# A group's state update moved directly ahead of its local products, in one unit, and the copy of its transposed k moved up to the transposes

## The chip, the cores and the metric

The program runs on one core of a Trainium2 chip. The metric is device time in microseconds (us), median of the runs shown. Five engines work side by side, each taking its own queue of instructions in order: TensorE (PE, matmuls; PEld is its weight loads), VectorE (DVE), ScalarE (ACT), GpSimd (POOL) and SyncE (SP, which here issues most DMA transfers). An instruction that waits holds everything behind it in its queue.

## The reference

Inputs q, k, v and f_logit have the shape (4, 8, 768, 48): batch, heads, tokens, head width. A gated recurrence runs over the tokens, and two MLPs with 384 inputs, 2048 hidden values and 384 outputs follow on all 3072 tokens.

```python
f = 1.0 / (1.0 + np.exp(-f_logit))
for t in range(S):
    state = f[:, :, t, :, None] * state + np.einsum('bhd,bhe->bhde', k[:, :, t], v[:, :, t])
    y[:, :, t] = np.einsum('bhd,bhde->bhe', q[:, :, t], state)
...
h = x @ w_in;  g = softplus(h);  x = g @ w_out           # first MLP
h = x @ w_in2; g = h * tanh(softplus(h)); x = g @ w_out2  # second MLP
```

## The kernel before

**The recurrence in groups.** The 768 tokens are cut into 6 chunks of 128. A group `g` is one chunk of one batch entry with all 8 heads, taken as 4 pairs; there are 24 groups, `g = 4 * chunk + batch`. For each group the kernel does, in this order:

- `a_scan`, `a_inv`, `a_q`, `a_k`, `a_decay` (lines 253 to 304, DVE and ACT): the running products of the gates, and q, k and the old state scaled by them (L256, L279 and L280, L286, L292, L300);
- `a_scores` (L322, PE): k times q within the chunk, into two PSUM banks; `a_mask` (L335, DVE): the causal mask, one bank at a time;
- `a_turn` (L346, PE): four transposes of the scaled k into a PSUM bank; `a_turned` (L352, ACT): the copy of that bank to the tile `kn`, which has one buffer;
- `a_out` (L390 and L399, PE): the local products (masked scores times v, L390) and the old state times q (L399); `a_outed` (L426 and L433, ACT): the copies of the result out of PSUM;
- `a_state` (L361, PE): `kn` times v, eight small matmuls; `a_stated` (L370, DVE): the new state, old plus product. The groups of the last chunk have no state to hand on, so 20 of the 24 groups have these two;
- `a_load` (SP): q, k and v of the group after next.

All PSUM banks that the steps of a group use are taken in turn from two (`ps_a`, tags a0 and a1, one buffer each): two for the scores, then one for each of the other PE steps in the order in which they are written.

**The MLPs in units.** A unit `(layer, k, f)` is one tile of 512 tokens (`k`, six of them) and one slice of 128 of the hidden values (`f`, sixteen), so there are 96 units per layer. `m_h` makes the hidden values (L483: nine matmuls of 512 columns, each product of two floats split into high and low parts, xh, xl and a two-part weight; the first eight slices of the first tile go whole, L469). Softplus or mish runs on ACT and DVE (L512 to L533), the result is split again (L498 `ghi`, L503 `glo`), and `m_o` multiplies it back (L613: six matmuls with `ghi`, three with `glo`; L603 whole). `m_o` follows three units behind `m_h`. The weights are split on the core too: `split_w` (L139 to L151) reads two loads of a slice (`raw`, L128 and the same bytes shifted, L129) and writes the high part at L147 and the low part at L151. For the first layer's slices 8 to 15 this stands in the units just ahead of their use; slices 14 and 15 take over the staging tiles of slices 12 and 13, once these are split.

**What sets the order.** The recurrence is woven into the first 80 units: `plan_attn` hangs the steps of a group on hooks of three units in a row, `at(unit, place, step)`, and a unit runs its places in the order act0, pe1, dve1, (softplus), act, (softplus), dve2, (split, `m_o`), pe2. That is the order in which the program is written. For these units the queue of each engine is then laid out by the framework's scheduler, which takes ready instructions by that order with times of its own, so a moved step can change the order of other work as well. From unit 80 on the order of PE, DVE and ACT is as written. The first four groups stand in a list of their own (`HEAD`) ahead of all units.

Of the kernel before, what the change touches and what calls it, by code (L numbers as in the profile page):

```python
# [17 lines left out]
B, H, S, D = 4, 8, 768, 48  # L18
C = 128
NC = S // C  # L20
# [38 lines left out]
def recurrence__then__softplus_mish_mlps_kernel(  # L59
# [43 lines left out]
    act, dve, pe = nc.scalar, nc.vector, nc.tensor  # L103
# [549 lines left out]
    def at(i, place, fn, *args):  # L653
        hooks.setdefault((i, place), []).append(lambda: fn(*args))
# [16 lines left out]
    def plan_attn(g, i):  # L671

        at(i, "pe1", a_scores, g)
        at(i, "dve2", a_mask, g, 0)
        at(i, "dve2", a_mask, g, 1)
        at(i + 1, "pe1", a_turn, g)
        at(i + 1, "act", a_turned, g)
        at(i + 1, "pe2", a_out, g)
        at(i + 2, "act0", a_outed, g)
        if g < (NC - 1) * B:  # L680
            at(i + 2, "pe1", a_state, g)
            at(i + 2, "dve2", a_stated, g)
        if g + 2 < NC * B:
            at(i + 2, "dve2", a_load, g + 2)

    for k in range(1, n1):
        c, b0, nb = tiles[1][k]
        base = (k - 1) * NF
        for j in range(nb):
            g, i = c * B + b0 + j, base + 3 * j  # L690
            plan_attn(g, i)
            if g + 1 < NC * B:
                plan_prep(g + 1, i if j < nb - 1 else i + 3)
            else:
                at(i + 3, "dve1", judge)
        i = base + 3 * nb
        at(i, "act", a_fill, k)
        for kk in range(KD):
            at(i + 1 + kk, "dve1", split_x, (1, k), kk)
# [20 lines left out]
    for f in range(NF):  # L720
        if f >= READY:
            i = f - AHEAD
            at(max(i - EARLY, -1), "act0", load_w, 1, f)
            at(i, "dve1", whole_w if f < NAT else conv1, f)
        i = first + SPAN + (last - first - SPAN) * f // NF
# [15 lines left out]
    for step in LOADS.split():  # L741
        what, g = step[0], int(step[1:])
# [333 lines left out]
```

## Time and profile before

| | us |
|---|---|
| median of 3 runs | 948.49 |
| lowest and highest | 948.35 and 949.86 |
| the profiled execution | 948.94 |
| its span (first to last instruction) | 947.2 |

| engine | busy us | share of the span |
|---|---|---|
| PE | 922.5 | 97% |
| PEld | 727.1 | 77% |
| DVE | 784.7 | 83% |
| ACT | 738.2 | 78% |
| POOL | 29.5 | 3% |

A busy time is the union of an engine's instructions. Matmuls are pipelined: one is shown from its start to a modelled end, which lies past the start of the next. So time lost between matmuls without a wait doesn't show as idle time; it is read from the distance of one start to the next.

### The profile page before, as it was taken

To read this page: it belongs to the slowest core of one execution; us is meant where nothing else is said; L and a number is where in the kernel's file an instruction comes from. 1 tells how busy PE (TensorE), PEld (TensorE's weight loads), DVE (VectorE), ACT (ScalarE), POOL (GpSimd) and SP (SyncE) were. 2 spreads that over 40 slices of the span, in tenths; PEclk is the share of its full clock that TensorE was granted. 3 is DMA by queue.
4 is the path that set the end of the run, shared out by engine and by line. 5 is a ranking of instruction groups with operands and counts; after the bars stand their busy time and mean duration, and the time that the engine had idled before them with its cause. 6 is when DMAs were issued, how large, how long until landed. Compare 5 with 4: busy or idle time off the path is not lost.

```text
span 947.2 us, 13705 instructions
## 1 busy us (share of the span) xinstructions
PE 922.5 (97%) x4970; PEld 727.1 (77%) x4970; DVE 784.7 (83%) x1252; ACT 738.2 (78%) x1326; POOL 29.5 (3%) x84
## 2 busy tenths in 40 slices
PE   4999989999999999999999999999999999999996
PEld 4655767787777777877888888888888888888885
DVE  5999999998998998987676688788877877877875
ACT  3778897888688787867687588787878878877875
POOL 1000000000000000000012210000000000000000
PEclk9999999999999999999999999999999999999999
DMA  9699713454754756381038660200200101000001
GB/s 307 226 354 332 272 56 110 131 196 174 246 177 159 267 183 215 144 283 42 9 135 261 178 226 1 67 34 1 88 13 27 74 1 67 34 1 1 34 0 38
DMA packets 35117, 122.33 MB, mean 129 GB/s; under 512 B 4352, under 2 KB 7424, under 8 KB 35040
## 3 DMA queue, kind: packets, MB, share of 16 engines
q1 hardware_dynamic: 28704, 99.34, 30.5%
q0 software_dynamic: 6336, 22.02, 7.2%
q8 instruction: 41, 0.67, 0.3%
q14 instruction: 36, 0.29, 0.1%
HBM read 93.62 MB, written 26.74 MB: 127 GB/s over the span
## 4 chain that ended last, share of the span: by engine, by line
PE 88%; DVE 7%; issue 2%; ACT 2%; POOL 0%; POOLq 0%; ACTq 0%; DVEq 0%
PE po L613 40%; PE ps L483 39%; PE ps L322 2%; PE ps L390 2%; PE ps L399 2%; PE ps L361 1%; PE ps L346 1%; PE ps L469 1%; DVE d L526 1%; PE busy L767 1%; DVE gg L256 1%; DVE a L335 1%; DVE w L147 1%; DVE d L520 1%; DVE raw L176 0%
## 5 line engine op out<-in xcount | busy, mean ns | idle before, releaser
L483 PE MATMUL ps<-x,w 128*128 128x512 f32 x864 | 214.0, 392 | 0.0
L613 PE MATMUL po<-ghi,w 128*128 128x512 f32 x768 | 206.7, 400 | 0.0
L483 PEld LDWEIGHTS ps<-x,w 128*128 128x128 f32 x864 | 162.3, 188 | 37.0
L483 PE MATMUL ps<-xh,w 128*128 128x512 f32 x528 | 181.3, 398 | 2.5 <-DVE w L151 2.3
L613 PEld LDWEIGHTS po<-ghi,w 128*128 128x128 f32 x768 | 141.5, 189 | 31.7 <-ACT ghi L498 0.7
L613 PE MATMUL po<-g,w 128*128 128x512 f32 x504 | 126.0, 394 | 0.0
L483 PEld LDWEIGHTS ps<-xh,w 128*128 128x128 f32 x528 | 98.9, 188 | 28.5 <-issue 3.6
L547 ACT ACTIVATE l<-d 128x512 f32<-128x512 f32 x96 | 60.7, 633 | 73.4 <-DVE d L543 73.4
L613 PE MATMUL po<-glo,w 128*128 128x512 f32 x384 | 112.4, 392 | 0.0
L613 PEld LDWEIGHTS po<-g,w 128*128 128x128 f32 x504 | 94.9, 188 | 21.4
L483 PE MATMUL ps<-xl,w 128*128 128x512 f32 x264 | 103.6, 392 | 0.0
L512 ACT ACTIVATE e<-ps 128x512 f32<-128x512 f32 x96 | 57.2, 596 | 56.6 <-PE ps L483 46.4
L503 DVE TENSOR_TENSOR glo<-l,ghi 128x512 fp32r<-128x512 f32 x128 | 87.7, 685 | 14.2 <-ACT ghi L498 13.6
L543 DVE TENSOR_SCALAR d<-ps 128x512 f32<-128x512 f32 x96 | 66.3, 690 | 37.5 <-PE ps L483 37.4
L498 ACT CAST ghi<-l 128x512 fp32r<-128x512 f32 x128 | 78.2, 611 | 20.7 <-DVE l L533 20.2
L557 DVE SCALAR_TENSOR_TENSOR l<-d,l 128x512 f32<-128x512 f32 x96 | 66.5, 693 | 33.2 <-ACT l L550 33.1
L520 DVE SCALAR_TENSOR_TENSOR d<-d,e 128x512 f32<-128x512 f32 x96 | 65.7, 685 | 23.1 <-ACT d L514 23.0
L613 PEld LDWEIGHTS po<-glo,w 128*128 128x128 f32 x384 | 72.4, 189 | 16.0
L580 DVE TENSOR_TENSOR l<-ps,l 128x512 f32<-128x512 f32 x96 | 66.4, 692 | 9.6 <-ACT l L577 0.9
L526 DVE TENSOR_TENSOR d<-l,d 128x512 f32<-128x512 f32 x96 | 65.7, 685 | 2.6
L572 DVE SCALAR_TENSOR_TENSOR l<-d,l 128x512 f32<-128x512 f32 x96 | 65.4, 681 | 0.0
L514 ACT ACTIVATE d<-e 128x512 f32<-128x512 f32 x96 | 60.7, 632 | 1.7
(107 smaller groups left out, 1284.4 us busy)
## 6 DMA issues: line engine op xcount, KB each, us to landing
raw<-in_w_dram SPq DMA_DIRECT2D x32, 768.0 KB, 6.1
w2d<-wo SPq DMA_DIRECT2D x32, 384.0 KB, 2.7
w<-w2d POOLq DMA_DIRECT2D x32, 384.0 KB, 3.9
raw<-in_w_dram SPq DMA_DIRECT2D x16, 767.9 KB, 10.4
win<-in_w_dram SPq DMA_DIRECT2D x16, 767.9 KB, 7.2
qk<-in_qkT_dram SPq DMA_DIRECT2D x22, 448.0 KB, 4.8
x2d<-o SPq DMA_DIRECT2D x12, 768.0 KB, 5.2
x<-x2d POOLq DMA_DIRECT2D x12, 768.0 KB, 5.4
```

Source lines behind the costliest of these rows:

```text
L483: pe.matmul(ps, w, r, start=(i == 0), stop=(i == len(steps) - 1))
L498: act.copy(out=t["hi"], in_=t["g"])
L503: dve.tensor_tensor(out=t["lo"], in0=t["g"], in1=t["hi"].bitcast(F32), op=ALU.subtract)
L514: act.activation(out=d, in_=e, func=AF.Identity, bias=1.0)
L520: dve.scalar_tensor_tensor(out=d, in0=d, scalar=1.0, in1=t["e"], op0=ALU.subtract, op1=ALU.subtract)
L526: dve.tensor_tensor(out=d, in0=l, in1=d, op=ALU.subtract)
L543: dve.tensor_scalar(out=t["t"], in0=t["h"], scalar1=20.0, scalar2=None, op0=ALU.min)
L547: act.activation(out=t["l"], in_=t["t"], func=AF.Exp)
L557: dve.scalar_tensor_tensor(out=t["l"], in0=t["t"], scalar=-43.0, in1=t["l"], op0=ALU.max, op1=ALU.add)
L572: dve.scalar_tensor_tensor(out=t["l"], in0=t["t"], scalar=-1.0, in1=t["l"], op0=ALU.mult, op1=ALU.max)
L580: dve.tensor_tensor(out=t["l"], in0=t["h"], in1=t["l"], op=ALU.mult)
L613: pe.matmul(acc[c], w[layer, f][:, cols[c]], t[part], start=(f == 0 and part == "hi" and w is whi), stop=(f == NF - 1 and part == "lo"),)
```

## The change

Three hooks of `plan_attn` move. The copy `a_turned` goes from the place act to the place pe1 of the same unit, right behind the transposes. `a_state` goes from pe1 of unit i + 2 to pe2 of unit i + 1, ahead of `a_out`. `a_stated` goes from dve2 to dve1 of unit i + 2.

```diff
         at(i + 1, "pe1", a_turn, g)
-        at(i + 1, "act", a_turned, g)
+        at(i + 1, "pe1", a_turned, g)
+        if g < (NC - 1) * B:
+            at(i + 1, "pe2", a_state, g)
         at(i + 1, "pe2", a_out, g)
         at(i + 2, "act0", a_outed, g)
         if g < (NC - 1) * B:
-            at(i + 2, "pe1", a_state, g)
-            at(i + 2, "dve2", a_stated, g)
+            at(i + 2, "dve1", a_stated, g)
```

No instruction is added or removed. The two PSUM banks change hands in another order: the state now takes the second bank of the scores, and the local products take the bank of the transposes, where before it was the other way round.

On PE around the local products of a group (here group 7), before: the products (L390, L399), a whole `m_h` (L483), then the state's matmuls (L361).

```order
L390 MATMUL ps<-a,vt 64x128 x8
L399 MATMUL ps<-qk,sp 48x128 x8
L483 MATMUL ps<-xh,w 128x512
L483 MATMUL ps<-xl,w 128x512
L483 MATMUL ps<-xh,w 128x512 x2
L483 MATMUL ps<-xl,w 128x512
L483 MATMUL ps<-xh,w 128x512 x2
L483 MATMUL ps<-xl,w 128x512
L483 MATMUL ps<-xh,w 128x512
L361 MATMUL ps<-vt,kn 64x48
L361 MATMUL ps<-vt,kn 48x48
```

And on PE at the same group now (three more pairs of L361 stand where lines are left out):

```order
L613 MATMUL po<-ghi,w 128x512 x6
L613 MATMUL po<-glo,w 128x512 x3
L361 MATMUL ps<-vt,kn 64x48
L361 MATMUL ps<-vt,kn 48x48
...
L390 MATMUL ps<-a,vt 64x128 x8
L399 MATMUL ps<-qk,sp 48x128 x8
L483 MATMUL ps<-xh,w 128x512
```

The eight small matmuls have moved from behind `m_h` to directly ahead of L390. From group 8 on this is so at eleven groups; at group 8 itself one of the eight stands alone, three L613 ahead of the other seven.

The second place is on PE at the last slice of the first tile (unit (1, 0, 15)), whose weights are split just ahead of it. Before: the `m_o` of slice 12, the nine L483 of slice 15, the `m_o` of slice 13.

```order
L613 MATMUL po<-ghi,w 128x512 x6
L613 MATMUL po<-glo,w 128x512 x3
L483 MATMUL ps<-xh,w 128x512
L483 MATMUL ps<-xl,w 128x512
L483 MATMUL ps<-xh,w 128x512 x2
L483 MATMUL ps<-xl,w 128x512
L483 MATMUL ps<-xh,w 128x512 x2
L483 MATMUL ps<-xl,w 128x512
L483 MATMUL ps<-xh,w 128x512
L613 MATMUL po<-ghi,w 128x512 x6
L613 MATMUL po<-glo,w 128x512 x3
```

And on PE there now:

```order
L613 MATMUL po<-ghi,w 128x512
L613 MATMUL po<-glo,w 128x512 x3
L322 MATMUL ps<-qk 128x128
L483 MATMUL ps<-xh,w 128x512
L483 MATMUL ps<-xl,w 128x512
L613 MATMUL po<-ghi,w 128x512 x6
L483 MATMUL ps<-xh,w 128x512 x2
L483 MATMUL ps<-xl,w 128x512
L483 MATMUL ps<-xh,w 128x512 x2
L483 MATMUL ps<-xl,w 128x512
L483 MATMUL ps<-xh,w 128x512
L613 MATMUL po<-glo,w 128x512 x3
```

Six L613 of slice 13 now stand between the second and the third L483 of slice 15, and the scores of group 8 (L322) are spread over this stretch in pieces of one, two, four and one, where before all eight stood together.

The third place is DVE at the same slice, around the last L151 with output `w`, which writes the low weights of slice 15. Before:

```order
L457 TENSOR_TENSOR xl<-x,xh 128x512
L148 TENSOR_SCALAR raw<-w 128x768
L533 SCALAR_TENSOR_TENSOR l<-ps,d 128x512
L151 SCALAR_TENSOR_TENSOR w<-raw 128x768
L457 TENSOR_TENSOR xl<-x,xh 128x512
L503 TENSOR_TENSOR glo<-l,ghi 128x512
L520 SCALAR_TENSOR_TENSOR d<-d,e 128x512
L457 TENSOR_TENSOR xl<-x,xh 128x512
L526 TENSOR_TENSOR d<-l,d 128x512
L199 TENSOR_TENSOR w<-w_346,w 128x768
L533 SCALAR_TENSOR_TENSOR l<-ps,d 128x512
L256 SCALAR_TENSOR_TENSOR gg<-f,cap 112x516
```

And on DVE there now:

```order
L526 TENSOR_TENSOR d<-l,d 128x512
L256 SCALAR_TENSOR_TENSOR gg<-f,cap 112x516
L457 TENSOR_TENSOR xl<-x,xh 128x512
L147 TENSOR_TENSOR w<-raw 128x768
L533 SCALAR_TENSOR_TENSOR l<-ps,d 128x512
L148 TENSOR_SCALAR raw<-w 128x768
L457 TENSOR_TENSOR xl<-x,xh 128x512
L151 SCALAR_TENSOR_TENSOR w<-raw 128x768
L503 TENSOR_TENSOR glo<-l,ghi 128x512
L520 SCALAR_TENSOR_TENSOR d<-d,e 128x512
L457 TENSOR_TENSOR xl<-x,xh 128x512
```

A scan (L256) and a second L457 now stand ahead of that L151. Counted from the start of the queue, these two are all that DVE does more before it than it did; every other kind of instruction comes as often.

## Rows read from the trace of the kernel before

**Rows 1.** The page, busy time of each engine.

```profile
PE 922.5 (97%) x4970; PEld 727.1 (77%) x4970; DVE 784.7 (83%) x1252; ACT 738.2 (78%) x1326; POOL 29.5 (3%) x84
```

**Rows 2.** Stretches of 25 us: PE, PEld, DVE, ACT, POOL busy (instructions), PEclk, DMA, GB/s.

```profile
75.00:100.00 25.00, 25.00 (x139) 14.21 (x137) 25.00 (x43) 20.07 (x33) 0.11 (x1) 1.00 1.01 325
125.00:150.00 25.00, 23.01 (x130) 17.70 (x129) 23.65 (x40) 19.78 (x37) 0.11 (x1) 0.93 0.16 57
```

**Rows 3.** PE's waits: waiting line, releaser: us in total, times, longest us.

```profile
PE ps L483 <- DVE w L151: 2.3, 2, 1.8
```

**Rows 4.** Timeline of PE, around group 9's state, then between tiles: start, us, what.

```profile
163.97 0.50 PE L483 MATMUL ps<-xh,w 128*128 128x512 f32 x1
...
166.24 0.67 PE L361 MATMUL ps<-vt,kn 128*64 128x48 f32 x16
166.83 1.65 PE L613 MATMUL po<-ghi,w 128*128 128x512 f32 x6
...
169.01 0.39 PE L483 MATMUL ps<-xh,w 128*128 128x512 f32 x1
...
203.27 0.39 PE L483 MATMUL ps<-xh,w 128*128 128x512 f32 x1
...
205.33 1.54 PE L613 MATMUL po<-ghi,w 128*128 128x512 f32 x6
```

**Rows 5.** Timeline of PE in the head, local products behind each other.

```profile
28.84 0.86 PE L413 MATMUL ps<-a,vt 128*48 128x128 f32 x12
29.53 0.64 PE L390 MATMUL ps<-a,qkv 128*64 128x128 f32 x4
...
30.97 0.86 PE L413 MATMUL ps<-a,qkv 128*48 128x128 f32 x12
31.76 0.94 PE L409 MATMUL ps<-y,sel 128*128 128x128 f32 x6
```

**Rows 6.** Instructions on line L361 from 130 to 460 us.

```profile
L361 PE MATMUL ps<-vt,kn x192: 208/222/257, 146.2 to 371.0; 128*64 128x48 f32 x96, 128*48 128x48 f32 x96
```

**Rows 7.** DVE's waits from 45 to 130 us, all there are.

```profile
DVE glo L503 <- ACT ghi L498: 0.2, 1, 0.2
```

**Rows 8.** Timeline, DVE and PE, up to the last slice of the first tile.

```profile
59.44 1.22 DVE L256 TENSOR_TENSOR_SCAN gg<-f,cap 112x516 f32<-112x516 f32 x1
60.58 0.53 DVE L163 TENSOR_SCALAR raw<-raw 128x768 int32<-128x768 int32 x1
...
129.25 0.68 DVE L457 TENSOR_TENSOR xl<-x,xh 128x512 fp32r<-128x512 f32 x1
129.39 0.73 PE L483 MATMUL ps<-xh,w 128*128 128x512 f32 x2 [1.80 <-DVE w L151]
129.85 0.68 DVE L503 TENSOR_TENSOR glo<-l,ghi 128x512 fp32r<-128x512 f32 x1
...
131.30 2.77 PE L613 MATMUL po<-ghi,w 128*128 128x512 f32 x6
...
134.75 0.40 PE L483 MATMUL ps<-xh,w 128*128 128x512 f32 x1
```

**Rows 9.** Timeline, slice 15's load and its first reader; then that load's landing.

```profile
113.61 0.94 DVE L151 SCALAR_TENSOR_TENSOR w<-raw 128x768 fp32r<-128x768 int32 x1
115.00 0.42 SPq L129 DMA_DIRECT2D raw<-in_w_dram  x1
123.43 0.56 DVE L140 TENSOR_SCALAR raw<-raw 128x768 int32<-128x768 int32 x1
...
DMA to landing us min/median/max: 7.1/7.1/7.1
```

**Rows 10.** Timeline, group 15's transposes, local products and copy.

```profile
278.62 0.55 PE L346 MATMUL ps<-ident,qk 112*128 112x112 f32 x4
281.17 1.09 PE L390 MATMUL ps<-a,vt 128*64 128x128 f32 x16
281.34 0.53 ACT L352 COPY kn<-ps 128x448 f32<-128x448 f32 x1
```

## The prediction

> **What bounds the kernel now.** I read the page's busy times first. PE is busy 97% of the span, DVE 83%, ACT 78% [rows 1], so the time is PE's unless another engine holds it up. Next PE's waits: from 50 us on there is hardly one, and the largest is for DVE, 2.3 us for the low weights that L151 writes [rows 3]. The table of stretches says where: from 75 to 100 us PE and DVE are both full; from 125 to 150 PE loses 2 us of 25 and its granted clock is 0.93 [rows 2]. So there are two regimes. Up to about 130 us DVE runs without a gap (its only wait from 45 to 130 us is 0.2 us, [rows 7]), and PE's work behind the last weight split can't start before DVE is through. From there PE never waits, and only what PE itself does counts.
>
> The Trainium skill says the same of the measure ("Perfetto Trace Analysis", Identifying the Most-Contended Engine): matmul busy time is a poor sign of distance to the limit. The trace agrees: weight loads are at 77% where matmuls show 97% [rows 1]. So I read starts, not busy times.
>
> **The change, part 1: the state's matmuls lose their own island.** Between tiles, where only matmuls of 512 columns run, nine take 205.33 - 203.27 = 2.06 us [rows 4]. The nine L483 between the local products and the state take 166.24 - 163.97 = 2.27, and the nine L613 behind the state 169.01 - 166.83 = 2.18 [rows 4]. Each side of an island of small matmuls costs about 0.1 us that no row shows as a wait. Before, the state (0.59 us from start to start) is an island of its own. Now it stands against L390, the two share their sides, and per group 0.10 (entering it) + 0.12 (leaving it) = 0.22 us goes.
>
> Then there is the joint L361 to L390, which the trace of before doesn't show. The nearest rows are in the head: twelve L413 take 29.53 - 28.84 = 0.69 us when L390 follows (both 64 columns or fewer wide) and 31.76 - 30.97 = 0.79 when L409 follows (128 wide) [rows 5]. L361 and L390 are of the first kind, so the end of L361 and perhaps the start of L390 each save some 0.1 or 0.05: between 0 and 0.15, I take 0.10, the nearest row. Per group 0.32 us, between 0.22 and 0.37.
>
> The Trainium skill gives a rule for this joint ("TensorEngine Tiling (Array Packing)", Key Properties): changing the tiling mode, not the tile, drains the engine. By it L361 (64 or 48 columns, all rows) to L390 (64 columns, all rows) drains nothing, and the upper figure would hold: 11 x 0.37 = 4.1 us. It has no price, and the sum stands on the rows.
>
> How many groups count? Behind 130 us there are 192 records of L361, 16 to a group, so 12 groups [rows 6]. In the new order one of the twelve (group 8) has one matmul left alone, which makes an island again. So 11 x 0.32 = 3.5 us less, between 2.4 and 4.1. The groups before 130 us save PE time too, but there PE only waits longer for DVE.
>
> **Part 2: the last weight split comes later.** DVE is dense, so its position is a sum. Ahead of the L151 of slice 15 stand one scan and one L457 more. A scan takes 60.58 - 59.44 = 1.14 us from start to start, an L457 129.85 - 129.25 = 0.60 [rows 8]: 1.74 us later. The state's L370 also moves forward, but it was ahead of that L151 already and costs nothing. It does add a wait of DVE for PE; the scheduler puts it behind the matmuls by about a DVE instruction, and where that fails L520 and the split behind it wait. I price this at 0.
>
> The loads come later too. Slice 15's second half is issued at 115.00, right behind the L151 that frees its staging tile (113.61 + 0.94), lands 7.1 us later at 122.1, and is read at 123.43: 1.3 us of slack [rows 9]. In the new order four more 512-column operations stand ahead of that freeing L151, 4 x 0.60 = 2.4 us (an L457's price), so landing is at 124.5. Its reader comes at about 124.2, by one more L520 and one L300 (0.9 or less). Cost 0.3 us, between 0 and 0.5. Sum of part 2: 2.0 us, between 1.7 and 2.3.
>
> **Part 3: what fills the wait.** Before, PE's third L483 of slice 15 starts at 129.39, after 1.80 us of waiting, and nine L613 follow [rows 8]. Now six of them stand ahead of that L483: 6 x 0.229 (2.06 / 9) = 1.38 us that no longer come behind it. That the scores of group 8 are cut into four pieces costs about 0.2 each, three more islands, but ahead of the wait, where it is covered: PE, 1.38 later by the six, still arrives before DVE, which is 2.0 later.
>
> **Part 4: the clock.** The nine L613 behind the wait take 134.75 - 131.30 = 3.45 us in place of 2.06 [rows 8], and the stretch has a granted clock of 0.93 [rows 2], a spell at 1.2 GHz in place of 2.4 that cost 25 x 0.07 = 1.75 us. PE had just waited 1.80 us. The new wait is of like size in sum, so I keep the cost; it could go (1.75 less) or come twice (1.75 more). The Trainium skill ("TensorE: Matmul & The Clock Gate", HAM oscillation) describes matmul bursts that run at half rate after each wait; the spell here agrees, and it speaks against a change that lengthens a wait.
>
> **Part 5: the copy.** The state now needs `kn` at PE's place of L390. In group 15 the transposes start at 278.62, L390 at 281.17, and the copy ends only at 281.34 + 0.53 = 281.87: 0.70 too late [rows 10]. Three more groups with a state were late so, by 0.2 to 0.35. With the old places of the copy PE would wait some 1.6 us in sum. In the new order of ACT the copy stands ahead of one or two casts or activations that it was behind in those four groups, about 0.5 us each, and for group 15 that is 0.2 short at most. I take 0, and 1.6 as the other end.
>
> **Sum.** -3.5 + 2.0 - 1.4 = -2.9 us. The profiled execution took 948.94, so 946.0; it lies 0.45 above the median of the runs shown, and against 948.49 the forecast is 945.6.
>
> **The rivals.**
> - *The islands were never worth so much, and the copy is late.* If the joint drains like any other (0.22 per group, -2.4) and the four groups wait (+1.6): -2.4 + 1.6 + 2.0 - 1.4 = -0.2, so 948.3; with one of the two, 946.7 to 947.2. For it: the joint is in no row, and the late copies are. Against it: the head's rows and the copy's new place. That the change then doesn't do what it says in time is this case.
> - *The half-rate spell goes.* The wait is cut in three (high weights, low weights, and slice 14's) with matmuls between. 945.6 - 1.75 = 943.9.
> - *Slower: the weights of slice 15 land late.* SP issues in order, and in the new order group 9's v load, which waits for group 7's local products, stands between the two halves of the load just ahead of slice 14's. If slice 15's load is put off by one whole landing, 7.1 us [rows 9], it lands at 129.2 in place of 122.1; its reader then starts 5.8 us after 123.43, the split behind it takes the rest of part 2's delay (1.74 - 0.9 = 0.8), and the whole is 6.6 us late where the forecast has 2.0. With a second spell: 945.6 + 4.6 + 1.75 = 952.0. It is slower than before from 2.9 us beyond the forecast on. Against it: by the sum above the first of these loads is issued when it was before, to within 2 us.
>
> **How the numbers follow.** About 0.2% (1.9 us) is what a measurement of this kernel can tell from no change. Forecast 0.50, half-rate spell gone 0.13, first rival 0.25, slower 0.12. Below 946.6 lie the forecast, most of its spread and the second rival: faster 0.62. Same takes the first rival and the forecast's upper edge: 0.27. Slower than 950.4: 0.11. The range runs from 943.6 (3.5 to 4.1 of islands, spell gone) to 948.7 (first rival and a little of the late weights); the forecast's own is 944.5 to 946.6.
>
> **What would show it.** Right: the nine L613 between a local product and the next L483 at 2.06 us in every group from 9 on; L361 followed by L390 at once; the L151 of slice 15 ending so that the third L483 of slice 15 starts 1.7 to 2.3 us after 129.39; PE's waits there 2 to 4 us. Wrong: a wait of L361 for the copy L352, a wait of DVE for `raw` loads before 130 us, a second spell of half clock, or new waits of PE behind 150 us, which would say that the new order of DVE or SP costs where PE was alone before.

## The result and the profile after

The changed kernel takes 954.08 us in the median of ten executions (952.01 to 957.16), the kernel before 948.42 (947.01 to 949.86) beside it. The ratio is 1.0062, 95% interval [1.0051, 1.0073]: it is 4.8 to 6.9 us slower where 2.9 faster was forecast. The profiled execution took 954.91, 5.97 more than that of before, with a span of 953.2. The busy times say almost nothing of it (the page after, as [rows 1]):

```profile
PE 921.5 (97%) x4970; PEld 726.0 (76%) x4970; DVE 783.6 (82%) x1252; ACT 741.3 (78%) x1326; POOL 30.4 (3%) x84
```

The list of PE's waits does (after; line, releaser: us in total, times, longest). `kn` is the copy of the transposed k, `ghi` the cast that `m_o` needs. These two are new; a wait for w was there before, of 2.3 us and for L151 [rows 3]:

```profile
PE ps L361 <- ACT kn L352: 4.5, 3, 1.7
PE po L613 <- ACT ghi L498: 3.3, 8, 0.7
PE ps L483 <- DVE w L147: 2.7, 1, 2.7
```

The stretches (after; columns as in [rows 2]) show the loss at slice 15 as before, with the clock at 0.93 again, and new losses behind it, where PE had been full:

```profile
125.00:150.00 25.00, 21.78 (x124) 16.79 (x124) 23.69 (x39) 22.24 (x40) 0.11 (x1) 0.93 0.15 52
275.00:300.00 25.00, 23.36 (x140) 18.75 (x141) 20.43 (x35) 19.20 (x36) 0.11 (x1) 1.00 0.52 180
350.00:375.00 25.00, 22.14 (x183) 17.56 (x182) 21.78 (x39) 18.08 (x34) 0.22 (x2) 1.00 0.43 151
```

PE's timeline after: slice 15's matmuls, group 9's joint island, the transposes of groups 13 to 15, and the state of group 15 (as [rows 4, 8, 10]):

```profile
128.21 0.50 PE L483 MATMUL ps<-xh,w 128*128 128x512 f32 x1 [2.70 <-DVE w L147]
128.55 0.39 PE L483 MATMUL ps<-xl,w 128*128 128x512 f32 x1
129.46 2.93 PE L613 MATMUL po<-ghi,w 128*128 128x512 f32 x6 [0.52 <-ACT ghi L498]
132.18 0.91 PE L483 MATMUL ps<-xh,w 128*128 128x512 f32 x2
...
161.38 0.61 PE L361 MATMUL ps<-vt,kn 128*64 128x48 f32 x15
...
162.86 1.08 PE L399 MATMUL ps<-qk,sp 48*48 48x128 f32 x16
163.87 0.50 PE L483 MATMUL ps<-xh,w 128*128 128x512 f32 x1
...
166.04 1.54 PE L613 MATMUL po<-ghi,w 128*128 128x512 f32 x6
...
168.10 0.39 PE L483 MATMUL ps<-xh,w 128*128 128x512 f32 x1
...
245.56 0.55 PE L346 MATMUL ps<-ident,qk 112*128 112x112 f32 x4
...
262.35 0.55 PE L346 MATMUL ps<-ident,qk 112*128 112x112 f32 x4
...
279.13 0.55 PE L346 MATMUL ps<-ident,qk 112*128 112x112 f32 x4
...
283.39 0.61 PE L361 MATMUL ps<-vt,kn 128*64 128x48 f32 x15 [1.64 <-ACT kn L352]
```

The island itself did what was forecast: the nine L613 take 168.10 - 166.04 = 2.06 us, and from one group's transposes to the next it is 16.79 (262.35 - 245.56), where before it was 278.62 - 261.49 = 17.13. So 0.34 us a group. The transposes of group 14 and the state of group 15 before ([rows 10] has the transposes of group 15):

```profile
261.49 0.55 PE L346 MATMUL ps<-ident,qk 112*128 112x112 f32 x4
...
285.47 0.67 PE L361 MATMUL ps<-vt,kn 128*64 128x48 f32 x16
```

But after the change the state waits 1.64 us for the copy of k. ACT's timeline says why (first after, then before; [rows 10] has the copy of before):

```profile
280.21 0.64 ACT L241 ACTIVATE f<-f 112x516 f32<-112x516 f32 x1 [0.96 <-DMA f<-in_fT_dram]
280.88 0.64 ACT L244 ACTIVATE f<-f 112x516 f32<-112x516 f32 x1
281.43 0.98 ACT L142 ACTIVATE raw<-raw,rebias 128x768 int32<-128x768 int32 x1
282.31 0.60 ACT L498 CAST ghi<-l 128x512 fp32r<-128x512 f32 x1
282.82 0.52 ACT L352 COPY kn<-ps 128x448 f32<-128x448 f32 x1
```

```profile
278.26 0.64 ACT L241 ACTIVATE f<-f 112x516 f32<-112x516 f32 x1 [0.16 <-DMA f<-in_fT_dram]
```

The copy is one place earlier in ACT's order than before (behind L498 instead of behind L498 and L512), but ACT is at L241 1.08 us after the transposes' start (280.21 - 279.13), where before it was 0.36 ahead of it (278.26 - 278.62). PE has gained; ACT, which waits for the load of f, has not come along. Of these 1.44 us, 1.0 is what PE gained since the start of the chunk (from the transposes of group 12 to those of group 15 it takes 50.38 us, before 51.38), and 0.4 is ACT itself standing later. The copy ends 3.66 us behind the end of the transposes (283.34 - 279.68). Before it was 2.70, harmless, since the state stood 6.3 us behind the transposes' end; its place is now 2.07 behind (283.39 - 1.64 - 279.68).

DVE's waits from 130 to 460 us have one new head, after:

```profile
DVE qk L286 <- DMA qk<-in_qkT_dram: 13.1, 8, 3.0
```

and before:

```profile
DVE qk L286 <- DMA qk<-in_qkT_dram: 0.7, 1, 0.7
```

Of the 5.97 us, by the starts of the transposes: -1.3 stand ahead of all groups (PE's first wait, in the head, is 11.9 in place of 13.1), +1.2 come up to group 8, +6.5 between groups 8 and 20 (262.63 where 256.14 were), -0.4 behind.

The listed waits understate this loss. Between groups 8 and 20 they are 7.4 us (4.5 for `kn`, 2.4 for `ghi`, 0.5 for the mask), and eleven joint islands give back 3.7, which leaves 3.7 of the 6.5. But a wait is counted from the modelled end of the matmul ahead of it. Here, after:

```profile
383.67 0.39 PE L483 MATMUL ps<-xh,w 128*128 128x512 f32 x1
384.39 1.66 PE L613 MATMUL po<-ghi,w 128*128 128x512 f32 x6 [0.33 <-ACT ghi L498]
```

The two starts lie 0.72 us apart where 0.23 is usual, and the next start comes 0.11 late, so a wait listed as 0.33 costs 0.60. With some 0.27 more for each of the six `ghi` waits in this stretch most of the gap closes.

### The profile page after: what moved, and what is told of

It reads as the page before. It is cut to its first block, busy times and chain, and to the rows that moved or that the text cites. A ratio compares the mean times of both kernels' runs of the same rounds, so it can differ in the third digit from the quotient of the medians.

```text
span 953.2 us, 13708 instructions
## 1 busy us (share of the span) xinstructions
PE 921.5 (97%) x4970; PEld 726.0 (76%) x4970; DVE 783.6 (82%) x1252; ACT 741.3 (78%) x1326; POOL 30.4 (3%) x84
## 4 chain that ended last, share of the span: by engine, by line
PE 72%; DVE 13%; DMA 5%; issue 4%; ACT 4%; SPq 0%; POOL 0%; DVEq 0%; POOLq 0%; ACTq 0%
PE po L613 33%; PE ps L483 32%; DMA qk<-in_qkT_dram 3%; DVE gg L256 1%; PE ps L322 1%; DVE d L526 1%; DVE d L520 1%; PE ps L390 1%; PE ps L399 1%; DMA x<-y 1%; DMA raw<-in_w_dram 1%; PE ps L469 1%; DVE a L335 1%; DVE l L533 1%; PE ps L361 1%
## 5 line engine op out<-in xcount | busy, mean ns | idle before, releaser
L483 PE MATMUL ps<-x,w 128*128 128x512 f32 x864 | 214.0, 392 | 0.0
L613 PE MATMUL po<-ghi,w 128*128 128x512 f32 x768 | 206.5, 399 | 3.3 <-ACT ghi L498 3.3
L483 PEld LDWEIGHTS ps<-x,w 128*128 128x128 f32 x864 | 162.3, 188 | 37.0
L483 PE MATMUL ps<-xh,w 128*128 128x512 f32 x528 | 181.3, 398 | 2.7 <-DVE w L147 2.7
L613 PEld LDWEIGHTS po<-ghi,w 128*128 128x128 f32 x768 | 141.7, 189 | 38.4 <-ACT ghi L498 7.7
L613 PE MATMUL po<-g,w 128*128 128x512 f32 x504 | 126.0, 394 | 0.0
L483 PEld LDWEIGHTS ps<-xh,w 128*128 128x128 f32 x528 | 99.2, 188 | 28.1 <-issue 3.8
L613 PE MATMUL po<-glo,w 128*128 128x512 f32 x384 | 112.6, 392 | 0.0
L613 PEld LDWEIGHTS po<-g,w 128*128 128x128 f32 x504 | 94.9, 188 | 21.4
L483 PE MATMUL ps<-xl,w 128*128 128x512 f32 x264 | 103.5, 392 | 0.0
L503 DVE TENSOR_TENSOR glo<-l,ghi 128x512 fp32r<-128x512 f32 x128 | 87.9, 686 | 14.3 <-ACT ghi L498 13.9
L498 ACT CAST ghi<-l 128x512 fp32r<-128x512 f32 x128 | 78.2, 611 | 26.3 <-DVE l L533 25.8
L512 ACT ACTIVATE e<-ps 128x512 f32<-128x512 f32 x96 | 57.2, 596 | 44.6 <-PE ps L483 27.2
L613 PEld LDWEIGHTS po<-glo,w 128*128 128x128 f32 x384 | 71.9, 188 | 16.5 <-DVE glo L503 0.9
L513 ACT ACTIVATE e<-e 128x512 f32<-128x512 f32 x96 | 60.7, 632 | 1.8
```

The costliest lines, as they stand in the source:

```text
L483: pe.matmul(ps, w, r, start=(i == 0), stop=(i == len(steps) - 1))
L498: act.copy(out=t["hi"], in_=t["g"])
L503: dve.tensor_tensor(out=t["lo"], in0=t["g"], in1=t["hi"].bitcast(F32), op=ALU.subtract)
L513: act.activation(out=e, in_=e, func=AF.Exp, scale=-1.0)
L613: pe.matmul(acc[c], w[layer, f][:, cols[c]], t[part], start=(f == 0 and part == "hi" and w is whi), stop=(f == NF - 1 and part == "lo"),)
```

## The experiments

Medians, ratios to the kernel before on the same chip, and of each profile PE's waits for kn and ghi and DVE's for q and k (these from 130 to 460 us). Runs on different chips are compared by their ratios.

The waits are those of one profiled execution, which is not always near the median: e1's took 952.91 us, e5's 953.19, e9's 956.45 and e14's 949.28. And in e15 to e18 9.1 to 9.7 us pass from the start of the last matmul to the end, before 7.7; so 1.4 to 2.0 us of their profiled times lie outside the stretch that they are about; the cause of that stays open.

| run | us (executions) | ratio, 95% | kn | ghi | qk |
|---|---|---|---|---|---|
| the change | 954.08 (10) | 1.0062 [1.0051, 1.0073] | 4.5 | 3.3 | 13.1 |
| e1 copy alone | 950.50 (12) | 1.0019 [1.0009, 1.0029] | 0 | 2.8 | 1.9 |
| e2 state behind | 951.73 (6) | 1.0036 [1.0021, 1.0050] | 0.2 | 3.9 | 8.9 |
| e3 v later | 952.96 (6) | 1.0047 [1.0033, 1.0062] | 4.6 | 2.7 | 10.4 |
| e4 q later | 958.05 (5) | 1.0093 [1.0077, 1.0109] | 10.9 | 1.0 | 8.4 |
| e5 copy back | 959.19 (6) | 1.0118 [1.0097, 1.0139] | 4.3 | 3.7 | 9.1 |
| e6 behind, copy back | 956.38 (5) | 1.0087 [1.0072, 1.0101] | 1.0 | 6.5 | 7.7 |
| e7 behind alone | 953.88 (6) | 1.0057 [1.0045, 1.0070] | 0.7 | 5.7 | 4.7 |
| e8 ahead alone | 953.24 (5) | 1.0048 [1.0035, 1.0061] | 4.8 | 3.8 | 6.0 |
| e9 ahead, old orders | 952.82 (5) | 1.0045 [1.0031, 1.0059] | 6.3 | 2.1 | 4.9 |
| e10 behind, old orders | 948.33 (12) | 1.0008 [0.9997, 1.0018] | 0 | 3.5 | 2.3 |
| e11 e9, copy earlier | 952.44 (5) | 1.0043 [1.0029, 1.0056] | 5.2 | 2.0 | 0.8 |
| e12 shorter m_o | 944.22 (5) | 0.9951 [0.9938, 0.9964] | 0 | 3.9 | 2.6 |
| e13 e10, v held | 949.56 (12) | 1.0012 [1.0002, 1.0021] | 0 | 3.4 | 2.9 |
| e14 e9, v held | 953.88 (6) | 1.0061 [1.0039, 1.0082] | 5.6 | 2.0 | 3.1 |
| e15 e10, stores on POOL | 955.70 (6) | 1.0073 [1.0055, 1.0092] | 0 | 2.5 | 1.4 |
| e16 e13, stores on POOL | 957.00 (6) | 1.0084 [1.0069, 1.0100] | 1.0 | 2.6 | 0 |
| e17 half the weights | 949.43 (11) | 1.0013 [1.0004, 1.0021] | 0 | 0 | 2.1 |
| e18 e17, state ahead | 950.00 (12) | 1.0023 [1.0013, 1.0033] | 3.4 | 1.0 | 6.9 |

**One part at a time (e1 to e4).** The first theory (A) was the loads: the state no longer holds v a unit longer, so the v load goes out beside that of q and k. Its rivals were the copy's place (B), the state's closeness to its copy (C), and products that end later and free q and k later (D). The edits, e1 against the kernel before, the others against the change:

```diff
e1:
-        at(i + 1, "act", a_turned, g)
+        at(i + 1, "pe1", a_turned, g)
e2 (the two change places):
         at(i + 1, "pe2", a_out, g)
+        if g < (NC - 1) * B:
+            at(i + 1, "pe2", a_state, g)
e3:
-            at(i + 2, "dve2", a_load, g + 2)
+            at(i + 2, "dve2", a_load if g < 2 * B else a_load_qk, g + 2)
+            if g >= 2 * B:
+                at(i + 3, "dve2", a_load_v, g + 2)
e4:
-        at(i + 1, "dve1", a_q, g)
+        at(i + 2 if g > 2 * B else i + 1, "dve1", a_q, g)
```

> Only the copy of the transposed k follows the transposes at once; the state matmuls stand one unit later ahead of the m_o half and the state add in dve2, as in the kernel before. Theory A (the q and k load that lands late is what the change costs, and it lands late because the v load now goes out just ahead of it): v is still freed a unit later here, so its load still follows the qk load, the DVE waits for qk stay under 2 us and the time is that of before, 948 to 949.5. Rival B (the copy, issued earlier in ACT's order, pushes the softplus steps that TensorE waits for): the waits of L613 for ghi, 3.3 us after the change, stay, and the time is 951 to 952. Rival C (the state matmuls two us behind their copy are the cost by themselves, through TensorE's waits for kn): no such wait here, 948 to 949.

Measured: 950.50, half a microsecond under B's range, and slower than before although PE's order is that of before, row for row. The one new entry among PE's waits in e1:

```profile
PE po L613 <- ACT ghi L498: 2.8, 5, 1.2
```

So a new order of ACT and DVE alone costs some 1.8 us here; of the three theories B comes nearest.

> The state matmuls stand directly behind the local products instead of ahead of them, in the same unit and the same island; all else as after the change. The copy gains the 1.15 us that the products take. Theory A: v is still freed with the products, its load still goes out with the qk load, so the DVE waits for qk stay near 13 us; TensorE's waits for kn fall from 4.5 us to about 2, and the time is 951 to 952.5. Rival C: the kn waits of 1.64, 1.11 and 1.74 us shrink to 0.5, 0 and 0.6, and the time falls by that 3.4 us alone, to 950 to 951; the qk waits stay but cost nothing. By rival B nothing moves but the kn waits as in C, while L613's waits for ghi stay at 3.3.

Measured: 951.73, kn waits 0.2, ghi 3.9, qk still 8.9. The kn waits went as C has it, and the time came down by about 2.4 us. That is less than the 3.4 of C, and the time lies in A's range.

> After the change, but from the third chunk of groups on the v load is issued one unit behind the qk load instead of with it (its buffer is free either way). Theory A: the qk load of 12 to 14 loads goes out alone again and lands in 3.5 to 4.2 us, the eight DVE waits for qk fall from 13.1 to under 5 us, the copy of the transposed k comes in time, TensorE's waits for kn (4.5) and for ghi (3.3) mostly go: 947 to 949.5. Rival D (the qk load is late because the products of two groups ago, which free its buffer, end later, not because of v): the waits for qk stay over 9 us, and the time at 953 to 954.5. Rival C: 953 to 954 as well, unless the kn waits go with them.

Measured: 952.96, qk 10.4. This one didn't do its edit in full: in six of the ten groups from 10 to 19 v still went out ahead of q and k, and in two more within 1.6 us behind. It says little on A; e13 and e14 do.

> After the change, but from the third chunk on the multiply of q by the decay (the first consumer of the qk load on DVE) stands a unit later, directly ahead of that of k; loads, buffers and TensorE's order are left (one xh matmul moves). Theory A and D alike (DVE stopping at the multiply of q is what makes ACT's copy and the softplus steps late): the waits for qk fall from 13.1 us to under 4, those of TensorE for kn and ghi from 7.8 to under 3, and the time to 947 to 950. Rival C (the kn waits come from ACT's own order, not from DVE): kn waits stay at 4 to 5 us and the time at 952 to 954. If the scores then wait for the later q, a new wait of L322 for L292 shows, of up to 1.1 us a group.

Measured: 958.05, above every range. The qk waits fell by 4.7 us, to 8.4 and not under 4, and the kn waits rose by 6.4. So fewer waits of DVE for q and k don't bring the copy in time, which speaks against A and D as the whole cause; a clean test it isn't, since most of the qk waits stayed.

**The parts undone (e5 to e8).** The edits: e5 and e6 put the copy back in act (in the change, and in e2); e7 and e8 move only `a_state` in the kernel before, behind and ahead of `a_out`.

```diff
e5, e6:
-        at(i + 1, "pe1", a_turned, g)
+        at(i + 1, "act", a_turned, g)
e7 (e8: the two lines ahead of a_out):
         at(i + 1, "pe2", a_out, g)
+        if g < (NC - 1) * B:
+            at(i + 1, "pe2", a_state, g)
...
-            at(i + 2, "pe1", a_state, g)
```

> The change without the move of the copy: the state matmuls stand directly ahead of the local products and the state add in dve1, as after the change, but the copy of the transposed k follows softplus's first activations again, as before; TensorE's order is that of the change but for one m_h matmul. Theory B (the copy that stands earlier on ACT delays the casts ghi, which cost the copy-only kernel 2.7 us of TensorE's waits and 1.8 us of time): the ghi waits fall from 3.3 us to under 1. Theory C (the state matmuls stand too close behind their copy): the kn waits grow, from 4.5 us in 3 groups to 6 to 9 in most. Together 953 to 957. If B alone holds, 950.5 to 952; if a reordering of ACT and DVE costs this much whatever the place of the copy, ghi and kn waits stay as they are and the time at 953 to 955.

Measured: 959.19 and ghi waits of 3.7. PE's order in the profile is that of the change, so B fails here: with the copy back in its old place the kernel is 5 us slower still. (The profiled execution is the fastest of the six.)

> As the kernel with the state matmuls directly behind the local products (951.7 us, kn waits 0.2, ghi waits 3.9), but with the copy of the transposed k back in its old place on ACT. The saving of the joint island stays, some 0.3 us in 20 groups. By theory B the ghi waits go from 3.9 to under 1 us; by C the state has 1.15 us more for its copy than in the change, and the four latest copies of the kernel before (lags of 2.2 to 2.7 us against the some 2.1 us to the products and 3.2 to the state) cause kn waits of under 0.5 us in all: 946.5 to 949. If ghi waits do not depend on the copy's place: 951 to 952 again.

Measured: 956.38, ghi 6.5. A miss, on the slow side.

> The least that gives the joint island: before, with only the state matmuls moved, directly behind the local products of the unit before; the copy and the state add in their old places. Saves as before some 0.3 us in 20 groups on TensorE. By theory B and C ghi and kn waits are as before (under 1 us): 944 to 947. If every reshuffling of the DVE and ACT orders costs 2 to 3 us by itself, 948 to 950.

Measured: 953.88, ghi 5.7, the longest 3.6 us. A miss again, 3.9 us above the higher of the two ranges.

> The change with only the state matmuls moved (directly ahead of the local products); copy and state add in their old places. Theory C: the copy is late by its old place, kn waits in most groups, 6 to 9 us, so 951 to 956, ghi waits under 1 us. If the state add in dve1 (directly after the half unit's start, ahead of the softplus of DVE) is what delays the softplus chain, this kernel has none of that and comes out under 950.

Measured: 953.24, in C's range, but with kn waits of 4.8 where 6 to 9 were expected and ghi waits of 3.8 where under 1 were. The state's move alone costs nearly what the change costs.

Every edit so far reshuffled the scheduler's orders of ACT, DVE and the DMA queue, in e7 for instance hundreds of rows. So the next four hold these orders. They weigh two more theories: F, that these new orders are what the change costs, and E, that between the first and the last group ACT, DVE and their loads set the pace, so that time saved on PE comes back as waits.

**The orders held (e9 to e12).** The rows of each queue for the first 80 units were written down from the kernel before and put back with edges between neighbours of one engine, which set the issue order and wait for nothing. No run holds them with nothing else changed, but the edges seem to cost nothing in this stretch: e17, which leaves PE's work and order alone, takes 256.00 us from group 8 to group 20, the kernel before 256.14.

```diff
+    for engine, order in ORDER.items():
+        pinned(engine, *order)
...
+                tc.add_manual_dep(i, prev.name, NoSync, reason="order")
```

In e11, ACT's table has the copy one row earlier at 19 of 20 places. In e12, PE's table is that of before, and

```diff
-        steps += [(c, whi, "lo") for c in range(KD)]
+        steps += [(c, whi, "lo") for c in range(KD - (layer == 1 and k in (1, 2, 3, 4) and 0 < f < NF - 1))]
```

> TensorE's order is that of the kernel before with only the eight state matmuls of a group put directly ahead of its local products, as in the change; the orders of DVE, ACT and the DMA queue are held, row for row, to those of the kernel before (edges that set the issue order and wait for nothing). It differs from the kernel with the state alone ahead (953.2 us) only in those orders. Theory F (what the change costs is not the state's place but the new orders that the scheduler gives DVE, ACT and the queue, in which the casts ghi and the copy kn come late): the ghi waits fall to under 0.5 us, the kn waits to what the old lags give (2.30, 2.71, 2.21 and 2.37 us against some 2.06 to the state's place, so about 1.5 us with a late q and k load on top), some 4 to 5 us of islands are saved: 945 to 947. Theory E (between the first and the last group DVE, ACT and their loads set the pace, so that TensorE's saved time comes back as waits whatever the order): 948 to 950, with new waits on TensorE that add up to the islands saved. Theory C (state too close behind its copy): as F, but kn waits of 4 us and more, 948 to 950.

Measured: 952.82, above every range and as slow as with the scheduler's orders (e8; the intervals overlap). F falls for the state ahead; the kn waits are as C has them. The profiled execution is the slowest of the five and holds a second spell at half clock, at 200 us. PE's waits in e9:

```profile
PE ps L361 <- ACT kn L352: 6.3, 6, 2.0
PE po L613 <- ACT ghi L498: 2.1, 2, 1.1
```

> As the last, with the state matmuls directly behind the local products; all other orders held to those of the kernel before. Theory F: the copy has 1.15 us more, so hardly any kn waits: 943.5 to 945.5, faster than both kernels. Theory E: 948 to 949.5. Theory C: as F.

Measured: 948.33, ratio [0.9997, 1.0018]: no change. No kn wait is left. Two things follow. Against e9, the same orders with the state on the other side of the products, the place ahead costs 4.5 us by the medians and 3.5 by the ratios. And against e7, the same place with other orders, the scheduler's orders cost 4.6 us by the ratios, so F holds there; from 156 us on PE's order is the same in both, and from group 8 to group 20 the profiles take 262.33 and 257.43 us. The PE time saved came back. In e10, ACT and then PE at the end of the chunk:

```profile
374.75 0.90 ACT L139 ACTIVATE raw<-raw 128x768 f32<-128x768 int32 x1 [2.67 <-DMA raw<-in_w_dram]
376.28 1.02 ACT L142 ACTIVATE raw<-raw,rebias 128x768 int32<-128x768 int32 x1 [0.63 <-DVE raw L141]
377.18 0.61 ACT L498 CAST ghi<-l 128x512 fp32r<-128x512 f32 x1
...
383.12 0.60 ACT L498 CAST ghi<-l 128x512 fp32r<-128x512 f32 x1
```

```profile
377.85 1.66 PE L613 MATMUL po<-ghi,w 128*128 128x512 f32 x6 [0.65 <-ACT ghi L498]
...
383.78 1.42 PE L613 MATMUL po<-ghi,w 128*128 128x512 f32 x5 [1.52 <-ACT ghi L498]
```

ACT stood 2.67 us for the raw half of a weight slice, and the casts behind it were late for PE.

> As the kernel with the state ahead and the old orders, but the copy of the transposed k stands one softplus activation (some 0.53 us) earlier on ACT in 19 of its 20 places; nothing else moves. Theory F and C: kn waits of under 0.5 us are left, 944 to 946, about 1 us under the one without. Theory B (the copy's earlier place makes the casts ghi late by itself): the ghi waits come back at 2 us and more, 947 to 949.

Measured: 952.44, above every range; the kn waits fell by 1.1 us and the median did not move. Half a microsecond is not what the copy lacks. This profile has no second spell, and from group 8 to group 20 it takes 258.91 us, 1.5 more than e10's.

> The kernel before in its own orders, with one of the nine matmuls of the second product (the last one, of the low half of g and the last third of the columns) left out in 56 units of the stretch of the groups: part of the result is not computed. TensorE has 56 times 0.213 us, 11.9 us, less to do; DVE, ACT and the queue do the same in the same order. It measures what a microsecond saved on TensorE is worth in this stretch. Theory F (with the old orders TensorE alone sets the pace): 936.5 to 939. Theory E: 945 to 948.5, the rest coming back as waits for ghi, kn, w and scores.

Measured: 944.22, ratio [0.9938, 0.9964], between the two ranges and nearer to E's. Of 11.9 us that PE has less to do, 3.4 to 5.9 arrive. PE's waits from 130 to 460 us, none of which the kernel before has:

```profile
PE po L613 <- ACT ghi L498: 3.9, 4, 1.8
PE ps L346 <- DVE a L335: 1.4, 1, 1.4
```

The lengths of the three chunks, from the starts of the transposes of groups 8, 12, 16 and 20, show where:

| | groups 8 to 12 | 12 to 16 | 16 to 20 |
|---|---|---|---|
| before | 86.06 | 85.12 | 84.96 |
| the change | 87.69 | 86.19 | 88.75 |
| e1 | 86.95 | 86.31 | 87.42 |
| e9 | 90.28 | 84.94 | 87.69 |
| e10 | 85.20 | 85.34 | 86.89 |
| e12 | 83.80 | 84.34 | 84.15 |
| e17 | 86.06 | 84.97 | 84.97 |
| e18 | 85.77 | 84.95 | 84.61 |

e9's first chunk holds the second spell. In e12 three matmuls less bring the distance between undisturbed groups from 17.13 to 16.46 us, 0.22 each, so each chunk has 14 x 0.22 = 3.1 us less on PE; it is 2.3, 0.8 and 0.8 shorter. What follows group 20, with 14 matmuls left out too, is no shorter (549.95 us, before 549.93). So theory E holds in the main: ACT, DVE and their loads have 2.3 us of room in the first of these chunks and 0.8 in the others, and what PE saves beyond that it waits. Which of the three sets this pace is not separated.

**What fills ACT and DVE (e13 to e18).** e13 and e14 let 16 of the v loads also wait for the matmul ahead of the state's old place; e15 and e16 move the stores of the second layer's weights (G: loads stand behind stores that wait for DVE); e17 and e18 leave out every second of these slices.

```diff
e13, e14:
+        tc.add_manual_dep(load, at_line[line][n].name, Sync, reason="hold")
e15, e16:
-            nc.sync.dma_start(out=w2d[f, z].bitcast(F32), in_=both[z].bitcast(F32))
+            nc.gpsimd.dma_start(out=w2d[f, z].bitcast(F32), in_=both[z].bitcast(F32))
e17, e18:
+        if f % 2 == 0:
             at(i - LEAD, "act0", load_w, 2, f)
             at(i, "dve2", conv_away, f)
```

> As the kernel with the state behind the products and all other orders as before (948.3 us, no gain for 0.21 us less a group on TensorE), but the v load of 16 groups also waits for the matmul that stood ahead of the state's old place, so that it goes out no earlier than before. Theory A (the v load that goes out with the raw half of the weights and with q and k delays them, and through ACT's and DVE's first steps on the weights the casts ghi): the ghi waits at the ends of the third and fourth chunk (0.61 and 2.17 us) go, 945 to 946.5. Theory E (ACT, DVE and the loads pace the stretch, v or no v): ghi waits of 2 us and more stay, 947.5 to 948.7.

Measured: 949.56, 0.9 above E's range, with ghi waits of 3.4 as in e10. A falls.

> As the kernel with the state ahead of the products and all other orders as before (952.8 us, kn waits 6.3 us), with the v load of 16 groups held to the state's old place. Theory A: the q and k loads land earlier, the copy's lag falls to those of before, kn waits under 2 us: 946 to 948. Theory E and C: the kn waits stay at 4 us and more, since the copy stands behind ACT's other work which does not speed up with TensorE: 950.5 to 953.

Measured: 953.88, 0.9 above the range of E and C, with kn waits of 5.6. A falls here too.

> State behind the products, orders of before, v not held, but the 32 stores of the converted second-layer weights go out from the POOL queue instead of the queue of the loads, so that a load no longer stands behind a store that waits for DVE. Theory G (the loads' place in the queue behind the waiting stores is what holds ACT and DVE back): q and k go out within 0.1 us of the end of their buffer's last reader instead of up to 3.6 us later, ghi waits under 1 us, 944.5 to 946. Theory E: nothing moves, 947.5 to 949.

Measured: 955.70, above every range, with a new wait of 3.5 us for glo (L503) at 398 us. That wait could hide a gain, but in the first two chunks, ahead of it, the time is that of e10 (85.19 and 85.12 us, e10 85.20 and 85.34). So G falls.

> Both of these: v held to its old time and the stores on the POOL queue. By theory A and G together 944 to 945.5, faster than the kernel before; by E 947.5 to 949.

Measured: 957.00, the same wait of 3.5 us.

> The kernel before in its own orders, with every second of the 16 slices of the second layer's weights left out of the conversion (their loads, the five DVE and two ACT steps and the two stores of each; the slice before is used in its place, so the result is another). That takes 28 us off DVE, 15 off ACT and 18 MB off the DMA engines between 200 and 440 us, and leaves TensorE its work. TensorE waits for nothing there in the kernel before, so by every theory 947 to 949; it is the measure for the next one.

Measured: 949.43, a little above the range. The chunks are those of before, and the excess lies behind the last matmul (9.1 us from its start to the end, before 7.7).

> The same, with the state matmuls directly ahead of the local products as in the change (orders otherwise as before; with all 16 slices this cost 4.8 us, with 6.3 us of kn waits and 2.1 of ghi waits). Theory E (ACT, DVE and the loads have no room for a TensorE that runs ahead; the conversion of the second layer's weights is what fills them): with half of it gone the kn waits fall under 2 us and the ghi waits under 0.5, and it is 2 to 4 us faster than the last one, 944 to 946. Theory C (the state's place, right behind its copy, is the cost whatever else runs): kn waits of 4 us and more stay, 949 to 952.

Measured: 950.00, beside 949.43 for e17, whose interval overlaps: with half of the conversions the state ahead costs 0.6 us (1.0 by the ratios) and not 4.8. But it gains nothing either: E's 944 to 946 is missed, and the time is one that C allows. PE's waits of e18 from 130 to 460 us:

```profile
PE ps L361 <- ACT kn L352: 2.8, 3, 1.2
PE ps L322 <- DVE state L370: 0.3, 1, 0.3
```

The ghi waits of the stretch are gone (the 1.0 us in the table lies at 118 us), as E had it, and the kn waits of the whole profile fell from 6.3 to 3.4, which lies between E's 2 and C's 4. DVE was busy 155.94 of the 170 us from 130 to 300 before, and 148.02 here (before, then e18; columns as in [rows 2]):

```profile
130.00:300.00 170.00, 170.00 (x1099) 134.52 (x1098) 155.94 (x257) 137.41 (x252) 0.90 (x8) 0.99 0.48 162
```

```profile
130.00:300.00 170.00, 167.85 (x1107) 134.70 (x1106) 148.02 (x243) 134.55 (x250) 0.90 (x8) 1.00 0.36 120
```

So E and C are both part of it: the state's place leaves the copy about 2 us, and a loaded ACT overruns them. A PE with less work and half of the conversions, which would test E more directly, was not run. No run with all of the work beats the kernel before.

## Why the prediction was wrong

**The bound.** The step that failed first is "From there PE never waits, and only what PE itself does counts". That PE doesn't wait was true; that a microsecond taken off PE is then a microsecond won was not. By e12 it is worth about two fifths (3.4 to 5.9 of 11.9). The row that could have warned is [rows 2] continued, the stretch of before that stands beside e18 above: DVE at 92% and ACT at 81% from 130 to 300 us, each in order, each with waits for loads.

**Part 1** held: 0.34 us a group in undisturbed pairs of groups, where 0.32 was forecast within 0.22 to 0.37. The rule of the Trainium skill ("TensorEngine Tiling (Array Packing)", Key Properties), that only a change of tiling mode drains, would have had the upper figure, 0.37; the measured one lies a little under it. Eleven such groups at 0.34 would have been 3.7 us.

**Parts 2 and 3.** Forecast +2.0 - 1.4 = +0.6 at slice 15. Measured +1.2 up to group 8, islands included. The load was the part mis-sized: DVE's reader of slice 15's second half waited 1.2 us for it, where 0.3 was allowed; the rival of the late weights, in small. After (DVE's line; then the load's landing):

```profile
123.93 0.56 DVE L140 TENSOR_SCALAR raw<-raw 128x768 int32<-128x768 int32 x1 [1.23 <-DMA raw<-in_w_dram]
DMA to landing us min/median/max: 7.8/7.8/7.8
```

It went out 2.4 us later, as forecast (116.1 where 115.0 was, with 1.3 us less in the head), but took 7.8 us to land and not 7.1. The six L613 did move ahead of the third L483, but into the half-rate spell and behind a wait of their own for ghi (0.52): they took 132.18 - 129.46 = 2.7 us and not 1.4. The third L483 starts 2.8 us behind 129.39, where 1.7 to 2.3 was the sign of being right, although the head is 1.3 us shorter.

**Part 4** held: one spell, 0.93 in the same stretch.

**Part 5** is the term that decided. Taken at 0 with 1.6 as the other end; the kn waits are 4.5 us, beyond both. The lags of the copy were read from a trace in which ACT keeps step with PE. After the change PE gains 0.34 us a group and ACT does not, so the lag grew from 2.70 to 3.66 us in group 15, and one place earlier on ACT (0.5 us) could not make that up. e9 against e10 gives the place ahead of the products, copy and bank together, as 3.5 to 4.5 us of time. In the change the products also take the bank of the transposes, so they wait for the copy too; which of the two matters was not tried.

**Left out** were the casts: 3.3 us of ghi waits from new orders of ACT and DVE that I had compared only at slice 15 and around the copy. e1 (+1.8 us with PE's order untouched) and e7 against e10 (4.6 us) show what such orders can cost. How the change's own 5.7 us divides between place and orders is not separated: e9 has 4.8 with the old orders, and its interval overlaps that of the change. The profiles allow an estimate, from one execution each: between groups 8 and 20 e11, with the place ahead and the old orders, takes 2.8 us more than the kernel before (258.91, 256.14), and the change 6.5; the other 3.7 would be the orders.

**Of the rivals**, the one that ended on the slow side came nearest in its number (952.0) and for the wrong reason; its load was 1.2 us late and not 5.8. The first rival had the right mechanism in one half, the late copy, at 1.6 us. Of the four signs that the prediction listed against itself, three came: the wait of L361 for the copy, DVE's wait for a raw load before 130 us, and new waits of PE behind 150 us.

**Open.** From execution to execution the change spreads from 952.0 to 957.2 us and e5 from 953.2 to 962.5, where the kernel before beside the change lies between 947.0 and 949.9. One profile of each doesn't show what differs.

## What to carry to other kernels

A busiest engine that never waits is not yet the only bound: shorten its work on purpose, with all other orders held, and see how much arrives before pricing an edit at its full worth. When an edit moves a consumer nearer to its producer on another engine, compare the producer's lag with the new distance after taking off what the consumer's engine gains, since the producer need not come along. And where a scheduler lays out the queues, hold the other queues' orders to tell an edit's own price from that of the reshuffle; here the reshuffle alone cost up to 4.6 us.

## What was not expected of the hardware

A wait of 2.0 us on PE, in e9, was followed by a stretch with a granted clock of 0.68 (200 to 210 us, where the kernel before has 1.00), in which the spell at 1.2 GHz lasted 6.8 us; so a wait can cost more than its length (in the spell at slice 15 after the change, six L613 took 2.7 us where 1.4 is usual):

```profile
200.00:210.00 10.00, 10.00 (x48) 7.86 (x46) 6.45 (x10) 4.73 (x9) 0.11 (x1) 0.68 0.49 165
```

The 1.80 us wait at slice 15, alike in twelve profiles, was followed by a spell of 3.4 us in nine and by none in three (e13, e14, e18). Six profiles (e4, e6, e7, e8, e15, e16) have another spell of 3.4 us, each behind a wait of 2.2 to 3.6 us, while a wait of 2.25 us in e3 and one of 2.02 in e4 had none behind them. And the first wait of PE in the head, with nothing changed there, ran from 11.9 to 13.5 us over the profiles and shifts all that follows.
